# Four small edits at the front of an attention and two-layer feed-forward kernel: group sizes, order of the last sums, a constant as a column, a rounding step on another engine

## The chip, the cores and the metric

The kernel runs on one core of a Trainium2 chip. A core has five engines, each with its own in-order queue of instructions: TensorE (PE in the profile; PEld is its weight load), VectorE (DVE), ScalarE (ACT), GpSimd (POOL) and SyncE (SP), which here issues nearly all DMA transfers. They meet only through semaphores. The metric is the device time of one execution in microseconds, as the median of several runs; lower is better.

## The reference

Everything is float32. With x of 12480 tokens by 128 features and 32 inducing rows I:

```
h   = softmax(I x^T / sqrt(128)) x            # 32 x 128, a sum over all 12480 tokens
a   = softmax(x h^T / sqrt(128)) h            # 12480 x 128; both softmaxes divide by (sum + 1e-9)
u   = a w1a ;  y = (u * clip(u + 3, 0, 6) / 6) w1b     # 128 -> 2048 -> 128
v   = y w2a ;  out = (max(v, 0)^2) w2b                 # 128 -> 2048 -> 128
```

The weights come as 64-bit floats, which the kernel turns into float32 itself (pieces a, b, c, d of 512 columns, four of each, for w1a, w1b, w2a, w2b).

## The kernel before, in words

**First attention, the front of the program.** The first softmax is a sum over all tokens, so nothing of the second may start before it is complete. The tokens are cut into nine groups (GROUPS, L31) of 4 times as many tokens as their blocks add up to: 1, 2, 3, 4, 4, 4 blocks of 128, then a group of 304 (kept for later use), then 3 blocks, then 1. For each group g the transposed tokens come by DMA (load_group, L340). PE makes scores (L400), DVE their negated maximum (L404), ACT the exponents (exps, L412) with their sum. For groups 0 to 5, PE turns the tokens block by block to rows (turn_x, L422; four transposes to a block) and ACT copies them out (L427). Groups 6 to 8 (NATURAL) are not turned: their rows are loaded a second time in natural order (load_natural, L357 and L361; n6, n7 and n8 below). PE turns the exponents (turn_e, L439; DVE copies them, L440), then sums rows weighted by exponents (accumulate, L450; four matmuls to a block), and ACT copies each group's sum to hsb (L455).

Each matmul in float32 shows as two passes in the trace: a row `x8` of L450 is one block.

**The end of the first attention.** The groups have their own maxima, so their sums are weighted: pl is the sum of lengths (L535), pg the weighted sum over groups 0 to 7 (L538), hg its copy on ACT (L543), ph the sum of the last group's part (L546) and of hg (L551). A few matmuls keep PE busy (fill, L290), DVE multiplies by the reciprocal (ht, L553), and the scores of the second attention follow (ps, L634).

**Queues around it.** SP issues the loads in the order of LOADS (L38): groups, pieces of w1a, then n6, n7, n8, pieces of w1b, and so on. The row tiles of natural loads share a ring of three buffers, so n7 waits until the sums of group 4 have been made; n7 and n8 are two halves of one tile.

**Second attention and feed-forward.** The 25 chunks of up to 512 tokens are worked through in stages k, eight to a chunk, written out in program order by the last loop (L919). In stage k PE makes two first-layer products (up1, L748), ACT the relu of h + 3 (L762), DVE the gate (L763), and PE, two stages later, the second product (down1, L790 or L802); the second layer follows 11 stages behind. The second softmax of chunk c + 1 is spread over the stages of chunk c: scores, att_shift, att_exp (ACT, L662), att_norm (DVE: l, le, r, a), att_turn. For chunks 0 and 1 att_norm also splits a into a rounded part (L687) and the rest (L690), both on DVE; PE turns them (L707) and ACT copies them out (L712). The norm of chunk 0 stands ahead of the stages, that of chunk 1 in stage 4. The turning of the weights (L180, L184 and L255 on ACT, L216 and L228 on DVE, L193 and L245 on POOL) lies between the stages by the tables EARLY, LATER and BESIDE.

Of the kernel before, what the change touches and what calls it, by code (L numbers as in the profile page):

```python
# [10 lines left out]
F32 = mybir.dt.float32  # L11
# [5 lines left out]
ALU = mybir.AluOpType  # L17
AX = mybir.AxisListType
# [3 lines left out]
P = 128  # L22
CH = 512
SHORT = {23: 384, 24: 320}
EPS = 1e-09
# [2 lines left out]
RAISED = {(kind, q) for kind in "bcd" for q in range(4)} | {("a", 3)}  # L28


GROUPS = [(128,), (128,) * 2, (128,) * 3] + [(128,) * 4] * 3 + [(128, 128, 48), (128,) * 3, (128,)]  # L31
KEPT = 6
TURN_V = {}
NATURAL = {6: (6,), 7: (7, 8), 8: ()}
AHEAD = 6


# [33 lines left out]
def induced_attention_then_two_ffn(  # L71
# [11 lines left out]
    nc = tc.nc  # L83
    NT, D = x.shape
    M = indT.shape[1]
# [6 lines left out]
    J = P // M  # L92
    SCALE = 1.0 / math.sqrt(D)
    NG = len(GROUPS)
    run = [sum(blocks) for blocks in GROUPS]
    assert sum(run) * J == NT and D == P and J == 4
# [18 lines left out]
    sp = ctx.enter_context(tc.tile_pool(name="sp", bufs=2))  # L115
# [150 lines left out]
    def jobs(names, engine=None):  # L266
        last = None
        for name in names.split():
            item, what = (name[0], int(name[1])), name[3]
            if what == "h":  # L270
                upper(item)
            elif what == "r":
                round_off(item)
            elif what == "l":
                last = lower(item, engine or nc.vector)
            elif what == "3":
                third_stage(item)
            elif what == "s":
                shift(item)
            elif what == "m":  # L280
                last = merge(item)
            else:
                last = (first_stage if what == "1" else second_stage)(item) or last
        return last

    def fill(n, pool, tag, bufs, of=None):
        t = pool.tile([P, P], F32, tag=tag, name="fill", bufs=bufs)
        for i in range(n):
            if of is None:
                nc.tensor.transpose(t, ident, ident)  # L290
            else:
                nc.tensor.matmul(t, lhsT=of, rhs=of, start=True, stop=True)
# [3 lines left out]
    def tick():  # L296
        ticks.append(len(ticks))
        return jobs(EARLY.get(ticks[-1], ""))
# [13 lines left out]
    xg = {}  # L312
    ctx.enter_context(tc.manual_schedule())
    with ExitStack() as pro:
        pp = pro.enter_context(tc.tile_pool(name="pp", bufs=1))
# [8 lines left out]
        sel, ind, inds = (row[:, i, :] for i in range(3))  # L324
        xn = {}

        def load_group(g):
            n = run[g] * J
            if g == KEPT:
                xg[g] = xlast  # L330
            elif g == 0:
                t = pp.tile([P, n + run[1] * J], F32, tag="x01", name="xg")
                xg[0], xg[1] = t[:, :n], t[:, n:]
            elif g == NG - 1:
                xg[g] = pp.tile([P, n], F32, tag="x01", name="xg")
            elif g > 1:
                xg[g] = pp.tile([P, n], F32, tag="xg", name="xg", bufs=3)
            if g == 3:
                nc.vector.tensor_copy(xg[g][:, :1], inds[:, :1])
            nc.sync.dma_start(xg[g], xT[:, t0[g]:t0[g] + n])  # L340
            of = NATURAL.get(g, (g,))
            if not of:
                return
            n = sum(len(GROUPS[i]) for i in of)
            t = pp.tile([P, n * J, D], F32, tag="xn", name="xn", bufs=3)
            for i in of:
                xn[i], t = t[:, :len(GROUPS[i]) * J, :], t[:, len(GROUPS[i]) * J:, :]

        def whole_blocks(g):
            return sum(blk == P for blk in GROUPS[g])  # L350

# [13 lines left out]
        def load(item):  # L365
            kind, n = item
            if kind == "x":
                load_group(n)
            elif kind == "n":
                load_natural(n)  # L370
            else:
                load_piece(item)
# [8 lines left out]
            out=sel, in_=ident.rearrange("p (j i) -> p i j", j=J), axis=AX.X, op=ALU.add  # L381
        )
        nc.vector.tensor_reduce(
            out=blk4, in_=ident.rearrange("p (j i) -> p j i", j=J), axis=AX.X, op=ALU.add
# [6 lines left out]
        hsb = pp.tile([P, NG, D], F32, name="hsb")  # L391
# [25 lines left out]
        def turn_x(g, b):  # L417
            blk, o = GROUPS[g][b], sum(GROUPS[g][:b])
            t = pps.tile([blk, J, D], F32, tag="xt", name="xt", bufs=4)
            for j in range(J):  # L420
                i = j * run[g] + o
                nc.tensor.transpose(t[:, j, :], xg[g][:, i:i + blk], ident)  # L422
            dst = xn[g][:blk].rearrange("p (j b) d -> p b j d", j=J)[:, b]
            if b in TURN_V:
                nc.vector.tensor_copy(dst, t)
            else:
                nc.scalar.copy(dst, t)  # L427

        def turn_e(g):
# [3 lines left out]
            for b, blk in enumerate(GROUPS[g]):  # L433
                o, full = sum(GROUPS[g][:b]), whole_blocks(g)
                if g in NATURAL and b < full:
                    e = es[g][:, b:full * P:full]
# [8 lines left out]
        def accumulate(g, first=0, end=J):  # L445
            nb = len(GROUPS[g])
            acc = hacc[g % 2][:, g // 2 % 4, :]
            for b, blk in list(enumerate(GROUPS[g]))[first:end]:
                for j in range(J):
                    nc.tensor.matmul(  # L450
                        acc[M * j:M * (j + 1), :], lhsT=et[g][:blk, b, M * j:M * (j + 1)],
                        rhs=xn[g][:blk, j * nb + b, :], start=(b == 0), stop=(b == nb - 1),
                    )
            if end >= nb:
                nc.scalar.copy(hsb[:, g, :], acc)  # L455
# [37 lines left out]
        for g in range(NG - 1):  # L493
# [9 lines left out]
            for b in range(len(GROUPS[g])):  # L503
                if g not in NATURAL:
                    turn_x(g, b)
# [21 lines left out]
        tick()  # L527
        accumulate(NG - 2)
        tick()
        accumulate(NG - 1)  # L530
        rw, lws = weights[1:]

        pg = pps.tile([P, D], F32, tag="xt", name="pg", bufs=4)
# [2 lines left out]
        for g in range(NG - 1):  # L536
# [3 lines left out]
                start=(g < J), stop=(g + J >= NG - 1),  # L540
            )
        hg = pp.tile([P, D], F32, tag="sel4", name="hg")
        nc.scalar.copy(hg, pg)  # L543
        tick()
        ph = pps.tile([P, M], F32, tag="xt", name="ph", bufs=4)
        nc.tensor.matmul(ph, lhsT=hsb[:, NG - 1, :], rhs=rw[:, NG - 1, :], start=True, stop=False)  # L546
        den = pp.tile([P, M], F32, name="den")
        nc.vector.tensor_scalar_add(den, pl, EPS)
        rec = pp.tile([P, M], F32, name="rec")
        nc.vector.reciprocal(rec, den)  # L550
        nc.tensor.matmul(ph, lhsT=hg, rhs=sel, start=False, stop=True)  # L551
        fill(5, pps, "xt", 4)
        nc.vector.tensor_tensor(  # L553
            out=ht4, in0=ph.unsqueeze(1).to_broadcast([P, J, M]),
            in1=rec.unsqueeze(1).to_broadcast([P, J, M]), op=ALU.mult,
        )
        jobs("b0.s")


    hp = ctx.enter_context(tc.tile_pool(name="hp", bufs=3, space=PSUM))  # L560
    ap_ = ctx.enter_context(tc.tile_pool(name="accp", bufs=1, space=PSUM))
    wpool2 = ctx.enter_context(tc.tile_pool(name="wpool2", bufs=1))
# [95 lines left out]

    def att_exp(c):
        t = att.pop(c)  # L660
        e = sp.tile(list(t.shape), F32, tag="e", name="e")
        nc.scalar.activation(e, t, AF.Exp, scale=SCALE)  # L662
        att[c] = e

    def att_weights(c):
        e = att.pop(c)
        shape = list(e.shape)
        l = sp.tile(shape[:2], F32, tag="l", name="l")
        nc.vector.tensor_reduce(out=l, in_=e, axis=AX.X, op=ALU.add)
        le = sp.tile(shape[:2], F32, tag="le", name="le")  # L670
        nc.vector.scalar_tensor_tensor(
            out=le, in0=l, scalar=EPS, in1=l, op0=ALU.add, op1=ALU.max
        )
        r = sp.tile(shape[:2], F32, tag="r", name="r")
        nc.vector.reciprocal(r, le)
        a = sp.tile(shape, F32, tag="a", name="a")
        nc.vector.tensor_tensor(
            out=a, in0=e, in1=r.unsqueeze(2).to_broadcast(shape), op=ALU.mult
        )
        return a  # L680

    def att_norm(c):
        a = att_weights(c)
        att[c] = a
        if c < TURNS:
            a4 = sp.tile([P, J, 2, 2, M], F32R, tag="a4", name="a4", bufs=1)
            nc.vector.tensor_copy(  # L687
                a4[:, :, :, 0, :], a.unsqueeze(2).to_broadcast([P, J, 2, M])
            )
            nc.vector.tensor_tensor(  # L690
                out=a4[:, :, :, 1, :], in0=a.unsqueeze(2).to_broadcast([P, J, 2, M]),
                in1=a4[:, :, :, 0, :], op=ALU.subtract,
            )
            att[c] = a4
            return a4[:, 0, 1, 1, :1].bitcast(F32)
        return a[:, 0, :1]
# [203 lines left out]
    jobs("b0.m")  # L900
    mix(0)
    att_exp(0)
    mix_high(0)
    mix(1)
# [14 lines left out]
    for k in range(K + OFF + L2 + 1):  # L919
        c, p = divmod(k, NP)  # L920
# [78 lines left out]
```

## Time and profile before

| what | before |
|---|---|
| time, median of 3 runs | 949.58 us (949.49 to 949.62) |
| the profiled execution | 949.87 us, of which the span is 948.1 us |
| PE busy | 941.7 us, 99% |
| DVE busy | 787.5 us, 83% |
| ACT busy | 818.2 us, 86% |
| POOL busy | 261.7 us, 28% |
| granted TensorE clock | full in every slice |

The span runs from the first instruction to the last; 1.8 us of the time lie around it. The time falls into a front of about 35 us (first attention, bound by loads and PE in turns), a run-in to about 63 us in which the stages of the first layer start, and a long even part. The profile's chain of waits follows the end of the program back to its start, at each step to what released it; a view by stretches gives the busy time of each engine, and a DMA view the time from issue to landing.

### The profile page before, as it was taken

What the parts mean: (1) busy time and instruction counts of PE and PEld (TensorE: products, weight loads), DVE (VectorE), ACT (ScalarE), POOL (GpSimd) and SP (SyncE); (2) the same over time, 40 slices, a digit from 0 to 9 for tenths busy, and PEclk for the clock granted to TensorE, in tenths of its full rate; (3) what the DMA queues carried; (4) which work ended last, traced back from release to release, by engine and by line L of the source; (5) the groups of instructions that cost most, each with busy time, mean ns of one, the idle gap of its engine ahead of it and who ended that gap; (6) DMA issues with size and microseconds to landing.
All of it is one profiled execution on the core that took longest, in us unless ns stands there. A gap on an engine that the chain in (4) does not pass through costs nothing.

```text
span 948.1 us, 12829 instructions
## 1 busy us (share of the span) xinstructions
PE 941.7 (99%) x4578; PEld 763.7 (81%) x4578; DVE 787.5 (83%) x948; ACT 818.2 (86%) x937; POOL 261.7 (28%) x427
## 2 busy tenths in 40 slices
PE   9999999999999999999999999999999999999998
PEld 6556788888888888888888888888888888888898
DVE  5898788888888888888888888888888888888774
ACT  6789888888888888888888888888888888889886
POOL 1356222222222222222222223222222222222222
PEclk9999999999999999999999999999999999999999
DMA  9731000002000002000000000010000100000000
GB/s 351 280 89 56 23 1 22 10 14 68 8 16 23 6 19 67 4 20 23 1 22 27 30 24 10 13 56 8 15 23 7 44 23 4 20 20 4 16 12 16
DMA packets 31424, 35.43 MB, mean 37 GB/s; under 512 B 7489, under 2 KB 24705, under 8 KB 30977
## 3 DMA queue, kind: packets, MB, share of 16 engines
q1 hardware_dynamic: 31216, 34.60, 11.0%
q8 instruction: 36, 0.59, 0.3%
q14 instruction: 28, 0.22, 0.1%
q10 hardware_dynamic: 144, 0.02, 0.0%
HBM read 22.33 MB, written 6.39 MB: 30 GB/s over the span
## 4 chain that ended last, share of the span: by engine, by line
PE 97%; DVE 1%; DMA 1%; ACT 0%; issue 0%; SPq 0%
PE h L831 28%; PE oacc L802 27%; PE yacc L802 26%; PE h L748 9%; PE yacc L790 2%; PE oacc L790 1%; DMA xg<-in_xT 1%; PE xt L422 1%; PE hacc L450 1%; PE ps L604 1%; PE s L400 1%; DVE g L763 0%; PE ett L439 0%; ACT g L762 0%; PE ps L634 0%
## 5 line engine op out<-in xcount | busy, mean ns | idle before, releaser
L763 DVE SCALAR_TENSOR_TENSOR g<-g,h 128x1024 f32<-128x1024 f32 (+3 forms) x201 | 238.7, 1189 | 116.6 <-ACT g L762 113.8
L762 ACT ACTIVATE g<-h,small 128x1024 f32<-128x1024 f32 (+3 forms) x201 | 219.3, 1092 | 107.1 <-PE h L748 106.7
L866 DVE TENSOR_TENSOR lo<-g,hi 128x1024 fp32r<-128x1024 f32 (+3 forms) x193 | 229.2, 1188 | 7.8 <-PE oacc L802 4.1
L782 DVE TENSOR_TENSOR lo<-g,hi 128x1024 fp32r<-128x1024 f32 (+2 forms) x186 | 221.1, 1189 | 0.8 <-POOL hi L774 0.8
L846 ACT ACTIVATE g<-g 128x1024 f32<-128x1024 f32 (+3 forms) x201 | 206.1, 1026 | 0.2
L842 ACT ACTIVATE g<-h 128x1024 f32<-128x1024 f32 (+3 forms) x201 | 199.2, 992 | 3.3 <-PE h L831 2.1
L858 ACT CAST hi<-g 128x1024 fp32r<-128x1024 f32 (+1 forms) x186 | 191.7, 1031 | 0.0
L774 POOL TENSOR_SCALAR hi<-g 128x1024 fp32r<-128x1024 f32 (+2 forms) x184 | 190.9, 1038 | 0.6 <-DVE g L763 0.2
L831 PE MATMUL h<-yh,wh 128*128 128x512 f32 (+2 forms) x400 | 153.8, 384 | 0.0
L831 PE MATMUL h<-yh,wl 128*128 128x512 f32 (+2 forms) x400 | 153.7, 384 | 0.0
L831 PE MATMUL h<-yl,wh 128*128 128x512 f32 (+2 forms) x400 | 153.7, 384 | 0.0
L748 PE MATMUL h<-at,m 128*128 128x512 f32 (+2 forms) x400 | 129.2, 405 | 0.6 <-DVE g L763 0.4
L895 POOL COPY small<-lo 128x1 f32<-128x1 f32 x115 | 21.8, 189 | 344.5 <-DVE lo L782 344.5
L802 PE MATMUL oacc<-hi,wh 128*128 128x512 f32 (+2 forms) x384 | 116.5, 384 | 0.0
L802 PE MATMUL oacc<-hi,wl 128*128 128x512 f32 (+2 forms) x384 | 116.4, 384 | 0.0
L802 PE MATMUL oacc<-lo,wh 128*128 128x512 f32 (+2 forms) x384 | 116.4, 384 | 0.0
L802 PE MATMUL yacc<-hi,wh 128*128 128x512 f32 (+2 forms) x372 | 112.4, 383 | 0.0
L802 PE MATMUL yacc<-hi,wl 128*128 128x512 f32 (+2 forms) x372 | 112.4, 383 | 0.0
L802 PE MATMUL yacc<-lo,wh 128*128 128x512 f32 (+2 forms) x372 | 112.4, 383 | 0.0
L748 PEld LDWEIGHTS h<-at,m 128*128 128x128 f32 x400 | 74.4, 188 | 24.8 <-issue 7.7
L831 PEld LDWEIGHTS h<-yl,wh 128*128 128x128 f32 x400 | 75.1, 188 | 14.5
L831 PEld LDWEIGHTS h<-yh,wh 128*128 128x128 f32 x400 | 75.1, 188 | 14.5 <-DVE g L763 0.4
(126 smaller groups left out, 912.9 us busy)
## 6 DMA issues: line engine op xcount, KB each, us to landing
outT<-osb SPq DMA_DIRECT2D x23, 256.0 KB, 2.2
xc<-in_xT SPq DMA_DIRECT2D x9, 512.0 KB, 4.3
xg<-in_xT SPq DMA_DIRECT2D x3, 1024.0 KB, 7.9
at<-ah SPq DMA_DIRECT2D x168, 16.0 KB, 1.8
at<-al SPq DMA_DIRECT2D x168, 16.0 KB, 1.8
raw<-in_w1a SPq DMA_DIRECT2D x4, 512.0 KB, 8.6
raw<-in_w1b SPq DMA_DIRECT2D x4, 512.0 KB, 7.5
raw<-in_w2a SPq DMA_DIRECT2D x4, 512.0 KB, 8.3
```

The source lines that it names most:

```text
L748: nc.tensor.matmul(h1[k][u] if k == 0 else h1[k][:, u, :size[c]], lhsT=m4[:, f * P:(f + 1) * P], rhs=a_t[c], start=True, stop=True)
L762: nc.scalar.activation(g, h, AF.Relu, bias=three)
L763: nc.vector.scalar_tensor_tensor(out=g, in0=g, scalar=6.0, in1=h, op0=ALU.min, op1=ALU.mult)
L774: nc.gpsimd.tensor_scalar(out=hi1[k], in0=g1[k], scalar1=1.0, scalar2=1.0, op0=ALU.mult, op1=ALU.mult)
L782: nc.vector.tensor_tensor(out=lo1[k], in0=g1.pop(k), in1=hi1[k], op=ALU.subtract)
L790: nc.tensor.matmul(acc, lhsT=w[:, f * P:(f + 1) * P], rhs=g[u] if isinstance(g, list) else g[:, u, :], start=(p == 0 and u == 0), stop=(p ...
L802: nc.tensor.matmul(acc, lhsT=w[:, f * P:(f + 1) * P], rhs=g[:, u, :], start=(p == 0 and n == 0), stop=(p == NP - 1 and n == 5),)
L831: nc.tensor.matmul(h2[k][:, u, :size[c]], lhsT=w, rhs=y, start=(n == 0), stop=(n == 2))
L842: nc.scalar.activation(g2[k][:, u, :], h[:, u, :n], AF.Relu)
L846: nc.scalar.activation(g2[k][:, u, :], g2[k][:, u, :], AF.Square)
L858: nc.scalar.copy(hi2[k][:, u, :], g2[k][:, u, :])
L866: nc.vector.tensor_tensor(out=lo2[k][:, u, :], in0=g[:, u, :], in1=hi2[k][:, u, :], op=ALU.subtract)
```

## The change

There are four edits.

1. GROUPS: the third group has two blocks instead of three, the last but one four instead of three. The natural rows of groups 7 and 8 no longer share a tile: group 8's rows lie behind its transposed tokens in a tile of the first groups' buffer.
2. The sums of the last group (accumulate of group 8) are written behind pg and hg instead of ahead of pl, and the two matmuls into ph change places.
3. In chunk 0 of the second attention the exponents lie in a tile with one more column that holds the constant 1e-9, and the reduction runs over it; the step that added the constant goes.
4. In chunk 1 the rounding of a is a copy on ScalarE instead of VectorE.

```diff
-GROUPS = [(128,), (128,) * 2, (128,) * 3] + [(128,) * 4] * 3 + [(128, 128, 48), (128,) * 3, (128,)]
+GROUPS = [(128,), (128,) * 2, (128,) * 2] + [(128,) * 4] * 3 + [(128, 128, 48), (128,) * 4, (128,)]
-NATURAL = {6: (6,), 7: (7, 8), 8: ()}
+NATURAL = {6, 7, 8}
...
             elif g == NG - 1:
-                xg[g] = pp.tile([P, n], F32, tag="x01", name="xg")
+                t = pp.tile([P, 2 * n], F32, tag="x01", name="xg")
+                xg[g], xn[g] = t[:, :n], t[:, n:].rearrange("p (b d) -> p b d", d=D)
...
-            of = NATURAL.get(g, (g,))
-            if not of:
-                return
-            n = sum(len(GROUPS[i]) for i in of)
-            t = pp.tile([P, n * J, D], F32, tag="xn", name="xn", bufs=3)
-            for i in of:
-                xn[i], t = t[:, :len(GROUPS[i]) * J, :], t[:, len(GROUPS[i]) * J:, :]
+            if g < NG - 1:
+                xn[g] = pp.tile([P, len(GROUPS[g]) * J, D], F32, tag="xn", name="xn", bufs=3)
...
-        accumulate(NG - 1)
         rw, lws = weights[1:]
...
         nc.scalar.copy(hg, pg)
+        accumulate(NG - 1)
         tick()
         ph = pps.tile([P, M], F32, tag="xt", name="ph", bufs=4)
-        nc.tensor.matmul(ph, lhsT=hsb[:, NG - 1, :], rhs=rw[:, NG - 1, :], start=True, stop=False)
...
-        nc.tensor.matmul(ph, lhsT=hg, rhs=sel, start=False, stop=True)
+        nc.tensor.matmul(ph, lhsT=hg, rhs=sel, start=True, stop=False)
+        nc.tensor.matmul(ph, lhsT=hsb[:, NG - 1, :], rhs=rw[:, NG - 1, :], start=False, stop=True)
...
+    e0 = sp.tile([P, J, M + 1], F32, tag="e", name="e0")
+    nc.vector.memset(e0[:, :, M:], EPS)
...
-        e = sp.tile(list(t.shape), F32, tag="e", name="e")
+        if c:
+            e = sp.tile(list(t.shape), F32, tag="e", name="e")
+        else:
+            e = e0[:, :, :M]
...
-        l = sp.tile(shape[:2], F32, tag="l", name="l")
-        nc.vector.tensor_reduce(out=l, in_=e, axis=AX.X, op=ALU.add)
         le = sp.tile(shape[:2], F32, tag="le", name="le")
-        nc.vector.scalar_tensor_tensor(
-            out=le, in0=l, scalar=EPS, in1=l, op0=ALU.add, op1=ALU.max
-        )
+        if c:
+            l = sp.tile(shape[:2], F32, tag="l", name="l")
+            nc.vector.tensor_reduce(out=l, in_=e, axis=AX.X, op=ALU.add)
+            nc.vector.scalar_tensor_tensor(
+                out=le, in0=l, scalar=EPS, in1=l, op0=ALU.add, op1=ALU.max
+            )
+        else:
+            nc.vector.tensor_reduce(out=le, in_=e0, axis=AX.X, op=ALU.add)
...
-            nc.vector.tensor_copy(
-                a4[:, :, :, 0, :], a.unsqueeze(2).to_broadcast([P, J, 2, M])
-            )
+            rounding = nc.scalar.copy if c else nc.vector.tensor_copy
+            rounding(a4[:, :, :, 0, :], a.unsqueeze(2).to_broadcast([P, J, 2, M]))
```

On PE, at the end of the first attention, the order before was this (hacc is the sums of L450, `x12` the three blocks of group 7, the `x4` behind it the block of group 8):

```order
L439 MATMUL ett<-ident,es 128x128
L450 MATMUL hacc_122<-xn,et 32x128 x12
L450 MATMUL hacc_121<-xn,et 32x128 x4
L535 MATMUL pl<-row,lws 128x32
L538 MATMUL pg<-hsb,rw 32x128 x8
L546 MATMUL ph<-rw,hsb 128x32
L551 MATMUL ph<-row,hg 128x32
L290 MATMUL fill<-ident 128x128 x5
```

In the changed program the same place on PE reads:

```order
L435 MATMUL ett<-ident,es 128x128
L446 MATMUL hacc_122<-xn,et 32x128 x16
L530 MATMUL pl<-row,lws 128x32
L533 MATMUL pg<-hsb,rw 32x128 x8
L446 MATMUL hacc_121<-xg,et 32x128 x4
L546 MATMUL ph<-row,hg 128x32
L547 MATMUL ph<-rw,hsb 128x32
L290 MATMUL fill<-ident 128x128 x5
```

Group 7 has a block more, the block of group 8 stands behind pg, and the part of hg now opens ph.

On ACT, in the stages around chunk 1's norm, the order before was this (g is the relu of a stage, stage 4 first; cva, cve and wh are steps of the weights; at is the turned a of chunk 1):

```order
L762 ACTIVATE g_737<-h_734,small 128x1024
L762 ACTIVATE g_756<-h_753,small 128x1024
L180 ACTIVATE cva<-raw 128x512
L184 ACTIVATE cve<-raw 128x512
L255 CAST wh<-w_642 128x512
L762 ACTIVATE g_778<-h_775,small 128x1024
L255 CAST wh<-w_680 128x512
L712 CAST at<-pt 128x512
```

In the changed program ACT has there:

```order
L765 ACTIVATE g_730<-h_727,small 128x1024
L692 CAST a_743<-a 128x8x32
L765 ACTIVATE g_749<-h_746,small 128x1024
L180 ACTIVATE cva<-raw 128x512
L184 ACTIVATE cve<-raw 128x512
L255 CAST wh<-w_635 128x512
L765 ACTIVATE g_771<-h_768,small 128x1024
L255 CAST wh<-w_673 128x512
```

The rounding of a stands behind the relu of stage 4 and ahead of that of stage 5 and the steps of the weights.

## Rows read from the trace of the kernel before

**Rows 1.** The page: busy time (share of the span) and instructions of each engine.

```profile
PE 941.7 (99%) x4578; PEld 763.7 (81%) x4578; DVE 787.5 (83%) x948; ACT 818.2 (86%) x937; POOL 261.7 (28%) x427
```

**Rows 2.** Stretches: length, then busy us of PE, PEld, DVE, ACT, POOL; clock, DMA.

```profile
52.00:56.00 4.00, 3.60 (x14) 1.99 (x13) 4.00 (x6) 3.23 (x6) 1.41 (x2) 1.00 0.11 22
56.00:60.00 4.00, 4.00 (x11) 1.78 (x10) 4.00 (x6) 2.68 (x5) 2.04 (x3) 1.00 0.85 238
100.00:200.00 100.00, 100.00 (x458) 80.39 (x457) 84.24 (x97) 86.33 (x93) 26.54 (x44) 1.00 0.06 17
```

**Rows 3.** The chain of waits in order of time: start us, us, what.

```profile
1.64 7.53 DMA xg<-in_xT
...
9.31 0.85 PE s L400 x8
...
10.53 1.31 PE xt L422 x12
...
30.40 1.01 PE hacc L450 x32
...
31.75 0.64 PE pg L538 x16
...
32.41 0.27 ACT hg L543
...
32.73 0.41 PE ph L551 x2
33.14 0.59 PE fill L290 x5
...
36.21 0.17 DVE le L671
...
51.22 0.59 DVE a L687
...
56.36 3.58 PE yacc L790 x8
```

**Rows 4.** SP's issues of n6's second part, then n7 and n8.

```profile
20.99 0.50 SPq L361 DMA_DIRECT2D xn<-in_x  x1
25.30 0.94 SPq L357 DMA_DIRECT2D xn<-in_x  x2
```

**Rows 5.** DMA issues: n7, and n6's second part; KB, us from issue to landing.

```profile
xn<-in_x SPq DMA_DIRECT2D x1, 768.0 KB, 4.5
...
xn<-in_x SPq DMA_DIRECT2D x1, 96.0 KB, 6.8
```

**Rows 6.** Stretches of one microsecond; the last two columns are DMA share and GB/s.

```profile
23.00:24.00 1.00, 1.00 (x15) 0.71 (x17) 0.93 (x3) 1.00 (x4) 0.00 (x0) 1.00 1.07 413
25.00:26.00 1.00, 1.00 (x16) 0.58 (x12) 0.40 (x2) 1.00 (x3) 0.17 (x1) 1.00 0.77 254
26.00:27.00 1.00, 1.00 (x11) 0.34 (x3) 0.88 (x2) 1.00 (x5) 1.00 (x1) 1.00 0.70 151
```

**Rows 7.** ACT in order of time: start, us, instruction, [idle before <- releaser].

```profile
35.54 0.31 ACT L662 ACTIVATE e<-t 128x128 f32<-128x128 f32 x1 [0.59 <-DVE t L653]
...
47.43 2.27 ACT L762 ACTIVATE g<-h,small 128x1024 f32<-128x1024 f32 x2
...
50.74 0.60 ACT L255 CAST wh<-w 128x512 fp32r<-128x512 f32 x1
...
53.09 0.58 ACT L712 CAST at<-pt 128x512 fp32r<-128x512 f32 x1 [0.23 <-PE pt L707]
54.22 1.11 ACT L762 ACTIVATE g<-h,small 128x1024 f32<-128x1024 f32 x1 [0.55 <-PE h L748]
...
58.61 1.14 ACT L255 CAST wh<-w 128x512 fp32r<-128x512 f32 x2 [1.10 <-POOL w L245]
```

**Rows 8.** DVE in order of time, the gates of stages 6 to 8.

```profile
54.25 1.21 DVE L763 SCALAR_TENSOR_TENSOR g<-g,h 128x1024 f32<-128x1024 f32 x1
...
56.69 2.34 DVE L763 SCALAR_TENSOR_TENSOR g<-g,h 128x1024 f32<-128x1024 f32 x2
```

## The prediction

> **What bounds the kernel now.** I read the page first: TensorE (PE) is busy for nearly the whole span [rows 1]. Then the table of stretches: from 100 us on PE works without a gap, while ScalarE (ACT) and VectorE (DVE) keep some 15% of slack, and the edits touch nothing there; between 52 and 60 us PE already loses 0.40 us, DVE is full, and ACT has 0.77 and 1.32 us idle [rows 2]. So a microsecond won or lost at the front goes one to one into the end. Third came the chain of waits in order of time [rows 3], which is where the terms are read: PE waits for the third group's load until 9.31, then works through to the sums that begin at 30.40, then the short pieces PE, ACT, PE that make h, a row of small DVE steps (le, a, ...), and a DVE stretch around 51 us before PE takes over again. Last I read the times of the natural loads [rows 4, 5], the DMA engines by microsecond [rows 6], and ACT and DVE around 50 us [rows 7, 8].
>
> **Part 1: third group of two blocks, last but one of four.** The load of x2 shrinks from 768 to 512 KB. Four transposes and one evacuation go (12 transposes take 1.31, so 4 take 0.44), and the sums of one block go (the row of 16 blocks' sums that follows 30.40 counts 32 passes, 8 to a block of four matmuls, so four blocks 1.01 and one 0.25) [rows 3]; group 7 gets that block's sums back. Through PE alone the sums of group 7 could begin earlier by 0.65 (x2, see below) + 0.44 + 0.25 + some 0.2 (an estimate: a third of the 0.85 that the third group's scores take, less about as much as group 7's grow by): 1.55 us, at 28.85 rather than 30.40.
>
> But group 7 isn't transposed: its rows come by a load of their own, which grows from 768 KB to 1 MB. It is 256 KB more in the one queue, and nothing ahead of it in the queue gets smaller in sum, because x7 takes back what x2 gives up. In the trace the part of n6 that was issued last (20.99) lands 6.8 later, at 27.79; n7, issued at 25.30, lands 4.5 later, at 29.80 [rows 4, 5]: 768 KB in 2.0 us behind n6, so 256 KB cost 0.65. Before, the sums wait 0.6 us beyond that landing, so it is hidden by that much only. From 25 to 27 us the queues run half empty (254 and 151 GB/s against 413 before), yet n6 still lands only at 27.8 [rows 6]: some of the 16 engines had finished and the last ones had not. The landing of n7 is that of the latest engine, which has no gap to fill, however early n7 is issued. So n7 lands at 29.80 + 0.65 = 30.45; with the 0.14 that lay between landing and first matmul for x2 (1.64 + 7.53 = 9.17, then 9.31 [rows 3]) the sums start at 30.59, 0.19 later than before. If instead the idle engines took the extra bytes, n7 would land at its old 29.8 and the sums start at 29.94. I take the first value, since n6 was late while engines stood idle.
>
> The Trainium skill, page "DMA: Bandwidth & Descriptors", section "Why a DMA increments its semaphore by 16 and not by 1", says that a transfer runs on up to 16 engines that finish independently and only the full count means that all has landed; the half-empty microseconds agree. The same page, "Measured (HBM→SBUF, 128 partitions, SWDGE, issued from GpSimd)", has the opposite pull: transfers of 1 MiB and more come nearer to peak, so four blocks would cost less than pro rata and two blocks more. No row here shows a gain by size in a full queue; by that rule the landing would move towards the second value.
>
> **Part 2: the last group's sums behind the weighted ones.** Counted from the start s of group 7's sums. Before: sums 1.01 (three blocks of group 7 and one of group 8), pl, then pg from s + 1.35 to s + 1.99, hg on ACT s + 2.01 to 2.28, ph until 33.14 = s + 2.74, the fills 0.59, next step at s + 3.37 [rows 3]. After: all four blocks belong to group 7 and stand ahead of pg, so pg still ends at s + 1.99; the block of group 8 (0.25) lies beside hg. That hides it, but its copy to SBUF on ACT now stands behind hg (s + 2.28 + 0.02 + 0.25 = s + 2.55) and the last ph matmul waits for it: s + 2.60 + 0.41 = s + 3.01. That is 0.27 later than before, which takes back all that the cover gives, so the added block is paid in full. n8 lands some 0.65 behind n7, before s + 1.99, so it isn't late; hsb of group 7 is ready while pg does its first seven matmuls. ACT's weight rounding queued behind that copy slides by the same amount; it ended 0.6 before the exponent, which waited for DVE that long, so it stays hidden.
>
> Front in sum: 0.19 + 0.27 = 0.46 us later at the first attention scores; −0.2 by the other value of the landing; −1.3 (28.85 − 30.40 + 0.27) if no load is late at all.
>
> **Part 3: the small constant as a column.** One DVE step on the chain goes: 0.17 + 0.02 = 0.19 us [rows 3]. Four more columns beside 128 lengthen the reduction by a thirtieth at most; the memset falls into DVE's wait for the scores. Bounds: −0.19, and 0 if the odd row pitch of e slows its three readers.
>
> **Part 4: second chunk rounded by ScalarE.** DVE loses a CAST of 0.59 [rows 3]. ACT gains one. Its price isn't in the trace for 256 columns: the exponent of 128 columns takes 0.31 and a CAST of 512 columns 0.60 [rows 7], so 0.41. What matters is its place. By the order it stands right behind the relu of stage 4 and ahead of the relu of stage 5. Its input a is ready on DVE at 51.2. Before, ACT ran two relus from 47.43 on (2.27 for both [rows 7]): the first ends at 48.55, the second is stage 5's, which DVE wants only after both of its rounding steps, the first of which ends at 51.81; then came weight rounding until 51.3 and stage 6's relu. After, ACT stands still from 48.55 to 51.2, 2.65 us, with all of that queued behind. Stage 5's relu starts at 51.2 + 0.41 = 51.6 instead of 48.57: ACT is 3.05 late. Its idle time from 52 to 60 is 0.77 + 1.32 = 2.09 [rows 2], so some 0.96 is left at 60 us. The path through DVE agrees: stage 7's relu moves from 54.22, less its wait of 0.55 and the 0.23 before it, by 3.05 to 56.5, ends at 57.6; DVE by then has done stage 6 (56.6 instead of 55.46 [rows 8]) and its two weight steps (55.46 to 56.69 before) at 57.85, does stage 7's product until 59.05 instead of 57.86, and PE's second half of the x8 row, which ended at 59.94 [rows 3], starts at 59.1 and ends at 60.9. I take +0.95. Bounds: below, −0.17, if ACT had nothing that anyone waits for (0.59 + 0.02 saved, 0.02 + 0.41 + 0.01 waited); above, the whole 3.05.
>
> **Sum against the profiled execution** (949.87 us, of which the span is 948.1 and 1.77 lies around it): 0.46 − 0.19 + 0.95 = +1.22. The median of the runs shown is 949.58, 0.29 below the profiled one; on it the forecast is 949.58 + 1.22 = 950.8 us. Less than about 0.2% (1.9 us) can't be told from no change, so the forecast is "same", on the slow side.
>
> **Rivals.**
> A. The extra natural bytes are taken by idle engines, n7 is in time; the rest as forecast: −0.2 − 0.19 + 0.95 = +0.56, 950.1. For it: the half-empty microseconds. Against: n6 lands late in spite of them.
> B. The lag of the latest engine is made during x2's load and goes with the smaller x2; no load is late: −1.3 − 0.19 + 0.95 = −0.54, 949.0. For it: at 0.65 per 256 KB the 1536 KB of x0 to x2 would take 3.9 us, and x2 lands only at 9.17, so some 3 us are lost there. Against: the bytes up to n7 are more, not fewer.
> C. ACT's standstill is free, because DVE is the bound of that stretch: 0.46 − 0.19 − 0.17 = +0.1, 949.7. Against: DVE itself needs the relu of stage 5 next. With B it would be −1.66, 947.9.
> D. The other side, slower by more than can be missed: ACT's standstill is not absorbed. Its idle stretches between 52 and 60 are waits for PE and GpSimd work that itself comes later, so they move along, and from 60 us on ACT has no slack that PE doesn't need. Then all 3.05 stay: 0.46 − 0.19 + 3.05 = +3.3, 952.9. It decides if PE still waits for stage 9's product when it comes back from stage 7. Against: stage 7 waited 0.55 for PE and a weight rounding 1.1 us for GpSimd, neither of which comes 3 us later.
>
> **How the numbers follow.** Forecast 0.50 (its own range 950.2 to 951.4: the landing 0.3 either way, the ACT term 0.5 to 1.4), A 0.20, B 0.08, C 0.08, D 0.12, something else 0.02. The forecast, A, C and most of B are within 0.2%; B with C is at the edge of faster; D and the upper tail are slower. Faster 0.03, same 0.84, slower 0.13. The range leaves out half of B and most of D: 949.2 to 952.2.
>
> **What would show it.** Right: x2 lands some 0.65 earlier and PE starts the third group's scores near 8.7; then PE idles ahead of group 7's sums with n7 as the releaser, landing near 30.4; ph's last matmul waits for ACT; no le step in the first chunk; an ACT gap of over 2 us ahead of the CAST, released by DVE a; DVE then waits for ACT's relu, and PE idles some 1 us more than before between 53 and 60. Wrong: group 7's sums start at 30 or earlier (A or B), no gap on ACT ahead of the CAST, or PE still behind by 3 us at 70 (D).

## The result: slower by 0.64%, outside the range

| | before | after |
|---|---|---|
| median, measured together (6 runs each) | 949.54 us (949.20 to 949.62) | 955.43 us (955.25 to 956.46) |
| ratio, 95% interval | | 1.0064 [1.0051, 1.0077] |
| profiled execution (span) | 949.87 us (948.1) | 956.46 us (954.7) |

The change costs 5.9 us by the medians and 6.6 us between the two profiled executions, of which the one after is the slowest of its six; 950.8 us was predicted, with 952.2 as the upper end. To find where the time goes, I take the start of ACT's relu of the same stage in both traces, each counted from the start of its span, after less before, and call it the shift. It is +0.29 us in stage 0, +3.24 in stage 5, +1.21 in stage 9, +1.20 in stage 14, +1.73 in stage 15, +1.71 in stage 23, +6.83 in stage 183 and +6.64 in the last. So there are three losses: 0.29 at the front, 1.45 at the run-in (0.92 until stage 9, 0.53 at stage 15), and 4.9 that come a little at a time in the even part. The first is within what the front varies by from one execution to the next (see the end of the experiments).

The page after, as [rows 1]: PE is as full as before, with 4 us more work by the clock and four instructions fewer.

```profile
PE 946.0 (99%) x4574; PEld 762.6 (80%) x4574; DVE 787.0 (82%) x947; ACT 818.4 (86%) x937; POOL 261.3 (27%) x427
```

**The front.** PE in order of time: the sums of group 7, with the idle time before them and its releaser.

```profile
30.55 0.71 PE L446 MATMUL hacc<-xn,et 128*32 128x128 f32 x17 [1.20 <-DMA xn<-in_x]
```

The chain of waits in order of time, as [rows 3]: start, us, what.

```profile
23.30 7.12 DMA xn<-in_x
...
30.55 1.08 PE hacc L446 x32
...
31.97 0.67 PE pg L533 x16
...
32.66 0.27 ACT hg L538
...
32.98 0.41 PE ph L546 x2
33.39 0.22 PE ph L547 x2
33.62 0.59 PE fill L290 x5
...
36.36 0.30 DVE le L677
...
36.69 0.19 DVE r L679
```

PE stands idle for 1.20 us until n7 lands at 23.30 + 7.12 = 30.42; ph now comes in two pieces, of which the second ends 0.48 us later than the one piece of [rows 3] (fill at 33.62 against 33.14); and in chunk 0 the reciprocal follows directly on the reduction.

**The run-in.** ACT in order of time, as [rows 7]:

```profile
47.73 1.13 ACT L765 ACTIVATE g<-h,small 128x1024 f32<-128x1024 f32 x1
51.52 0.40 ACT L692 CAST a<-a 128x256 fp32r<-128x256 f32 x1 [2.66 <-DVE a L681]
51.83 1.11 ACT L765 ACTIVATE g<-h,small 128x1024 f32<-128x1024 f32 x1
```

Between the relus of stages 4 and 5 ACT stands still for 2.66 us, until DVE has made a, and then rounds it. The table of stretches shows what PE loses by it, first before, then after (columns as in [rows 2]):

```profile
50.00:55.00 5.00, 4.60 (x16) 2.38 (x15) 4.83 (x11) 4.22 (x7) 1.82 (x4) 1.00 0.34 102
70.00:75.00 5.00, 5.00 (x18) 3.01 (x17) 3.94 (x5) 5.00 (x8) 3.89 (x5) 1.00 0.08 20
```

```profile
50.00:55.00 5.00, 4.10 (x15) 2.32 (x14) 3.84 (x9) 3.48 (x6) 1.70 (x2) 1.00 0.32 105
70.00:75.00 5.00, 4.50 (x14) 2.38 (x14) 4.39 (x8) 5.00 (x7) 3.26 (x6) 1.00 0.05 13
```

PE idles 0.90 us of the first stretch instead of 0.40, and 0.50 of the second, where before it was full.

**The even part.** One stage on PE begins with the pair of first-layer matmuls, `h<-at,m`. Before, two such pairs in sequence, and what follows the first:

```profile
402.41 0.62 PE L748 MATMUL h<-at,m 128*128 128x512 f32 x2
402.86 0.39 PE L831 MATMUL h<-yh,wh 128*128 128x512 f32 x1
...
404.22 0.61 PE L802 MATMUL yacc<-hi,wh 128*128 128x512 f32 x2
...
406.94 0.61 PE L748 MATMUL h<-at,m 128*128 128x512 f32 x2
```

The same after:

```profile
406.12 0.63 PE L751 MATMUL h<-at,m 128*128 128x512 f32 x2
406.59 0.39 PE L834 MATMUL h<-yh,wh 128*128 128x512 f32 x1
...
407.97 0.61 PE L805 MATMUL yacc<-hi,wh 128*128 128x512 f32 x2
...
410.69 0.63 PE L751 MATMUL h<-at,m 128*128 128x512 f32 x2
```

A stage takes 4.57 us instead of 4.53, with no idle time and the same instructions. All of it lies between the pair and yacc: 1.85 us (407.97 − 406.12) instead of 1.81. The groups of instructions between 200 and 800 us (busy us, mean ns of one), before and then after:

```profile
L748 PE MATMUL h<-at,m 128*128 128x512 f32 x262 | 81.2, 391 | 0.0
...
L831 PE MATMUL h<-yh,wl 128*128 128x512 f32 x262 | 102.0, 389 | 0.0
```

```profile
L834 PE MATMUL h<-yh,wl 128*128 128x512 f32 x262 | 103.5, 395 | 0.0
...
L751 PE MATMUL h<-at,m 128*128 128x512 f32 x261 | 82.5, 396 | 0.0
...
L805 PE MATMUL oacc<-hi,wh 128*128 128x512 f32 x260 | 80.0, 389 | 0.0
```

No edit touches these matmuls. What differs is where their operand lies: tile at is at byte 137728 of each partition before and at 137664 after, 64 bytes lower, by the addresses in the two built programs. Edit 3 is why: chunk 0 no longer takes a tile l, so the allocator first meets l in chunk 1 and puts it behind at instead of ahead of it. yh, yl, hi, lo and the weights lie where they lay. With 160 stages from 23 to 183, the growth of the shift, 6.83 − 1.71 = 5.12 us, is 0.032 a stage.

### The profile page after: what moved, and what is told of

Read it like the earlier page. It is cut to its first block, busy times and chain, and to the rows that moved or that the text cites. A ratio compares the mean times of both kernels' runs of the same rounds, so it can differ in the third digit from the quotient of the medians.

```text
span 954.7 us, 12817 instructions
## 1 busy us (share of the span) xinstructions
PE 946.0 (99%) x4574; PEld 762.6 (80%) x4574; DVE 787.0 (82%) x947; ACT 818.4 (86%) x937; POOL 261.3 (27%) x427
## 4 chain that ended last, share of the span: by engine, by line
PE 95%; DMA 2%; DVE 2%; ACT 1%; issue 0%; SPq 0%; ACTq 0%
PE h L834 28%; PE oacc L805 27%; PE yacc L805 26%; PE h L751 9%; PE oacc L793 1%; PE yacc L793 1%; DMA xg<-in_xT 1%; DVE g L766 1%; DMA xn<-in_x 1%; PE ps L602 1%; ACT g L765 0%; PE xt L418 0%; DMA row<-in_indT 0%; PE hacc L446 0%; PE s L396 0%
```

## The experiments

Every kernel below was timed against the kernel before on the same chip; three chips were used, so each time stands beside its own time before. Three things were to be told apart: whether the place of at is the cause of the loss in the even part, whether ACT's standstill is that of the run-in, and what the other edits do.

**The change with l kept in chunk 0**, which puts at back at 137728:

```diff
         le = sp.tile(shape[:2], F32, tag="le", name="le")
+        l = sp.tile(shape[:2], F32, tag="l", name="l")
         if c:
-            l = sp.tile(shape[:2], F32, tag="l", name="l")
```

> The changed kernel with one line more: the small tile l is also taken in chunk 0 (nobody uses it there), so that the tile at (the turned weights that the first-layer matmuls read) lies where it lay before, at byte 137728 of a partition, a multiple of 512, and not 64 bytes lower. Every instruction is the same. Theory P (place): in the changed trace each even stage is 4.567 us long against 4.533, all of the 34 ns in the eight matmuls from the two that read at; over some 155 stages that is 5.2 us. With at back the stage is 4.533 again and the time 955.4 - 5.2 = 950.2 us. Rival T (time): ACT's standstill put the engines out of step and the stages never come back into it; then the place does nothing and the time stays 955.4. Rival O: it is the order of e, nm and t, which this kernel leaves as changed; also 955.4.

Measured: 950.62 us against 949.26, ratio 1.0018 [1.0009, 1.0027]. The shift is constant, +0.75, from stage 17 to the end. The groups, 200 to 800 us:

```profile
L751 PE MATMUL h<-at,m 128*128 128x512 f32 x262 | 81.2, 391 | 0.0
```

The mean is that of before. A tile of 16 bytes that chunk 0 takes and doesn't use (with its second buffer and the spacing, 64 bytes) returns the even part; what is left, 1.36 us by the medians, is near the 1.22 that the prediction had for the whole change.

**The kernel before with l alone moved** out of its ring in chunk 0, so that at lies 64 bytes lower; no other line is changed (le, r, a, a4 and st, which stand between l's old place and its new one, move down with it):

```diff
-        l = sp.tile(shape[:2], F32, tag="l", name="l")
+        l = sp.tile(shape[:2], F32, tag="l" if c else "nm", name="l")
```

> The kernel before with the reverse: l takes, in chunk 0 alone, a buffer of nm's ring, so its own is first taken in chunk 1, behind at; at lies 64 bytes lower, at 137664, as in the changed kernel. No instruction changes. P: 949.5 + 5.2 = 954.7 us, stages of 4.567. T and O: 949.5 us.

Measured: 954.21 us against 949.26, ratio 1.0050 [1.0035, 1.0065]. The shift is +0.16 at the front, +0.21 in stage 15 and +5.12 at the end, so 4.91 come behind stage 15. Two pairs in sequence, and the group:

```profile
400.03 0.63 PE L748 MATMUL h<-at,m 128*128 128x512 f32 x2
...
404.60 0.63 PE L748 MATMUL h<-at,m 128*128 128x512 f32 x2
```

```profile
L748 PE MATMUL h<-at,m 128*128 128x512 f32 x260 | 82.1, 396 | 0.0
```

Stage length, mean and the 4.91 us are those of the changed kernel. So the move of these tiles alone makes the whole loss of the even part, without any of the four edits; at is the only one of them that the matmuls of an even stage read.

**Other distances.** l and le both moved (at 128 bytes lower), and a tile of 32 bytes that restores half of the distance (at 32 lower):

```diff
-        le = sp.tile(shape[:2], F32, tag="le", name="le")
+        le = sp.tile(shape[:2], F32, tag="le" if c else "nm", name="le")
```

> As the last one, with le moved likewise: at lies 128 bytes lower than in the kernel before, at 137600, a multiple of 128 but not of 256 or 512. P with a grid of 128 bytes or less: 949.5 us, stages of 4.533. P with a coarser grid (256 or 512): about 954.7 us again. T and O: 949.5 us.

```diff
-        l = sp.tile(shape[:2], F32, tag="l", name="l")
+        l = sp.tile(shape[:2], F32, tag="l" if c else "nm", name="l", bufs=1 if c else 2)
...
+            if c == 0:
+                gap = sp.tile([P, 8], F32, tag="gap", name="gap", bufs=1)
```

> The kernel before with at 32 bytes lower (l's own buffers behind at, one of them only, and an unused tile of 32 bytes ahead), at byte 137696. No instruction changes. Measured so far: 64 bytes lower makes an even stage 4.567 us and the time 954.2 (950.6 with at back), 128 bytes lower 4.553 and 952.2. P as 'any place off a multiple of 512 costs': a stage of 4.55 to 4.57 again, 951.5 to 954.5. P as 'only the 64-byte half counts, the 128 run was something else': 4.533 or 4.567, nothing between.

Measured: 952.18 us (ratio 1.0029 [1.0018, 1.0040]) at −128 and 952.82 (1.0035 [1.0022, 1.0048]) at −32; a stage takes 4.55 us in both. Every distance tried costs, and not in proportion to it: 64 bytes cost most.

**The second layer's tiles moved instead**, at left in place. A gap ahead of their pool moves yh, yl, g2, hi and lo of the second layer, by 64, 128 and 256 bytes:

```diff
+    gap = ep2.tile([P, 16], F32, tag="gap", name="gap", bufs=1)   # 16, 32 or 64 columns
     def up1(k):
```

> The kernel before with at in its old place, but all moving operands of the second layer (yh, yl, hi, lo) 64 bytes higher, by an unused tile ahead of them. If a place off the 512 grid slows any matmul that reads there, the twelve second-layer matmuls of a stage (six of h, six of oacc) slow down instead of the first ones: the two of at cost 34 ns, so twelve cost up to 200 ns a stage and the time is up to 30 us longer; slower by over 5 us in any case. If it is something of at alone (its DMA writers, say): 949.5.

> As the run with the second layer's moving operands 64 bytes higher (+13.7 us, stages 4.620), now 128. If the cost is that of a place off a multiple of 512: slower again, stages of 4.57 to 4.64, 955 to 965. If a multiple of 128 is enough: 949.7 (the 128-byte shift of at cost 20 ns a stage, which speaks against).

> The same with 256 bytes. Grid of 512: slower, stages over 4.55, 952 to 965. Grid of 256: 949.7, stages of 4.533.

Measured: 963.34 us at +64 (1.0145 [1.0131, 1.0159]), 961.91 at +128 (1.0135 [1.0122, 1.0149]) and 949.47 at +256 (1.0001 [0.9992, 1.0010]). The second layer's second product, between 200 and 800 us, at +64 and at +256:

```profile
L803 PE MATMUL oacc<-hi,wh 128*128 128x512 f32 x258 | 81.2, 396 | 0.0
```

```profile
L803 PE MATMUL oacc<-hi,wh 128*128 128x512 f32 x264 | 81.3, 389 | 0.0
```

So it isn't the move but the address: all operands that stream through these matmuls lay at multiples of 512 bytes, a shift by 256 is free, and every smaller one costs. It isn't particular to at either. At +64 a stage takes 4.62 us; 12 of its 20 matmuls read moved tiles, and the loss is 0.09.

**Edit 4 alone** in the kernel before:

```diff
-            nc.vector.tensor_copy(
-                a4[:, :, :, 0, :], a.unsqueeze(2).to_broadcast([P, J, 2, M])
-            )
+            rounding = nc.scalar.copy if c else nc.vector.tensor_copy
+            rounding(a4[:, :, :, 0, :], a.unsqueeze(2).to_broadcast([P, J, 2, M]))
```

> The kernel before with the fourth edit alone (chunk 1's rounding on ScalarE); at stays at 137728. By the prediction ACT stands still for 2.65 us and +0.95 us is left: 950.5. The changed trace lost 0.9 at stage 10 and 0.54 more at stage 16: if both come from the standstill, +1.45: 951.0. T: the stages get out of step and the even part drifts, some +5 to +6: 955. If ACT's standstill is absorbed: 949.4.

Measured: 950.33 us against 949.26, ratio 1.0011 [1.0002, 1.0021]. ACT and the two stretches:

```profile
46.34 1.11 ACT L761 ACTIVATE g<-h,small 128x1024 f32<-128x1024 f32 x1
50.11 0.40 ACT L688 CAST a<-a 128x256 fp32r<-128x256 f32 x1 [2.66 <-DVE a L677]
```

```profile
50.00:55.00 5.00, 4.09 (x14) 2.04 (x12) 3.89 (x6) 4.89 (x8) 1.79 (x3) 1.00 0.28 79
70.00:75.00 5.00, 4.51 (x16) 2.61 (x15) 3.74 (x5) 5.00 (x8) 3.86 (x5) 1.00 0.09 22
```

The same gap, and the same two losses on PE. The shift goes from −1.09 in stage 4 to −0.19 in stage 9 and +0.34 from stage 15 to the end: 0.90, then 0.53. In the even part it stays where it is. Both losses of the run-in are edit 4's.

**Edit 4 written later**: the same copy on ACT, but in stage 5, behind that stage's relu and two weight steps (att_round is att_norm from the rounding on). DVE's step that takes the rest of a goes along with it, and the weight step b3.2 now stands behind both.

```diff
+        if k == 5:
+            jobs("c0.1 b0.h")
+            att_round(1)
+            last = jobs("b3.2") or last
```

> The kernel before with the fourth edit at another place: chunk 1's rounding is on ScalarE, but written in stage 5, behind that stage's relu and two weight steps, where its input is ready when ACT comes to it; the rest (DVE) stands behind the gate of stage 5. ACT does the same work as in the run with edit 4 alone (+1.1). If the standstill is the cause: no gap ahead of the CAST, and 949.6, the time of before. If it is ACT's added work or PE's later turn: +1.1 again, 950.7.

Measured: 949.28 us against 949.40, ratio 0.9999 [0.9990, 1.0008]. ACT and the stretches:

```profile
49.52 0.60 ACT L255 CAST wh<-w 128x512 fp32r<-128x512 f32 x1
50.02 0.40 ACT L694 CAST a<-a 128x256 fp32r<-128x256 f32 x1
50.33 1.10 ACT L766 ACTIVATE g<-h,small 128x1024 f32<-128x1024 f32 x1
```

```profile
50.00:55.00 5.00, 4.85 (x17) 2.62 (x16) 5.00 (x8) 4.70 (x9) 1.91 (x4) 1.00 0.48 145
70.00:75.00 5.00, 4.99 (x18) 2.99 (x17) 2.95 (x4) 5.00 (x7) 3.33 (x5) 1.00 0.10 26
```

No gap, and PE full in the second stretch. In the profiled execution the shift even falls, from −1.24 in stage 4 to −1.59 in stage 9, and then stays; the medians don't show that 0.35. The copy's work on ACT costs nothing that can be seen; with its early place go the gap and a loss of 1.4 us within the profiled execution, 1.07 us by the medians. What the later DVE step and b3.2 do by themselves wasn't run.

**The other edits.** Edits 1 to 3 with l kept (the first experiment with the rounding back on DVE), edit 3 alone with l kept, and edit 3 with l kept together with edit 4 written later:

```diff
-            rounding = nc.scalar.copy if c else nc.vector.tensor_copy
+            rounding = nc.vector.tensor_copy
```

> The changed kernel with l taken in chunk 0 (at in its old place) and the rounding of chunk 1 back on VectorE: edits 1, 2 and 3 alone. By the prediction +0.46 from the natural load and the tail and -0.19 for the missing step: +0.27, 949.5. Rival A or B (n7 in time, lag gone): -0.4 to -1.5, 948 to 949. From the runs with at back (950.6) less what edit 4 cost alone (+1.1): about the time of before.

> The kernel before with the third edit alone, at in its old place: one DVE step of 0.19 us fewer on the chain. Prediction: -0.19, so 0.02% faster, at the edge of what can be seen among front-end differences of 1 us from run to run; the profile should show the stages 0.2 us earlier counted from the last ph matmul. If the odd pitch of e costs its readers: 0.

> The kernel before with the third edit and the fourth at its later place, at where it was: -0.2 for the missing DVE step, 0 to -0.2 for the rounding off DVE: 949.3, that is 0.03% faster, if anything can be seen of it.

Measured: 949.55 us against 949.67 (1.0004 [0.9993, 1.0016]; one of the eleven runs took 955.49), 949.41 against 949.67 (0.9996 [0.9987, 1.0005]) and 948.95 against 949.40 (0.9995 [0.9986, 1.0004]). None can be told from the kernel before; the last has the lowest median, and whether it is better stays open.

The front varies from one execution to the next, also where its code is the same. The chain of the kernel with edit 4 alone begins like this; [rows 3] has 7.53 for the same load.

```profile
1.64 6.00 DMA xg<-in_xT
7.64 0.14 issue
7.77 0.85 PE s L400 x8
```

No edit touches this load, yet it lands 1.5 us earlier, and the shift in stage 0 is −1.12. Two more traces hold the changed front, the change with l kept and edits 1 to 3: their shift in stage 0 is −0.69 and −0.36, where the changed kernel has +0.29. Medians of the kernel before went from 949.26 to 949.67 between the chips, single runs from 948.39 to 950.55. So terms of the front, 0.2 to 0.5 us, can't be read from the times, and of the traces only steps counted from the step before them, not from the start.

## Why the prediction was wrong

**The step that failed is Part 3.** It priced the constant's column by its instructions alone, between −0.19 and 0 us. The instruction did go and saved its 0.19. But the edit also drops a tile in chunk 0, the tiles behind it move down by 64 bytes, and the first-layer matmuls of all later stages slow down: 4.9 us, where the upper bound was 0. With it falls the sentence in the first part that from 100 us on the edits touch nothing: they change no instruction there, but an address. No rival held it, since all of them dealt with waits and landings; the range was built from those and so ended at 952.2. The list of the tiles' addresses in the two built programs, which needs no run, would have shown the move; its price took runs.

The Trainium skill, page "SBUF — State Buffer", section "Operand start alignment", asks of an operand's address only that it be a multiple of the element's size, and says of itself that this is about legality and not about speed. The runs agree, and add the price: every address tried was legal, and 5 of 6 were slower.

**Part 1's numbers came out, partly by luck.** n7 was put at 30.45 and landed at 30.42, the sums at 30.59 and began at 30.55. The argument was that idle engines take nothing, however early n7 is issued. But n7 was issued 2.00 us earlier than before (23.30 against 25.30), and the dip that the argument rests on [rows 6] shrank; after the change (columns as there):

```profile
25.00:26.00 1.00, 1.00 (x31) 0.80 (x34) 1.00 (x4) 0.97 (x3) 0.32 (x2) 1.00 0.94 261
26.00:27.00 1.00, 1.00 (x27) 0.80 (x16) 1.00 (x3) 0.67 (x3) 0.40 (x1) 1.00 1.05 389
```

The queues moved 261 and 389 GB/s there instead of 254 and 151, and n7 was late all the same. In the other two traces of this front, first the change with l kept, then edits 1 to 3, the sums of group 7 began at:

```profile
29.58 1.08 PE L446 MATMUL hacc<-xn,et 128*32 128x128 f32 x32 [0.84 <-DVE rw L484]
```

```profile
29.91 1.08 PE L446 MATMUL hacc<-xn,et 128*32 128x128 f32 x32 [1.17 <-DVE cve L228]
```

Each time that is 0.14 us behind n7's landing (29.44 and 29.77), as forecast, though in these two the profile names DVE as the releaser. But 29.94 was rival A's value, and in the eleven traces with the old front the sums begin anywhere from 28.99 to 30.45. So that PE idles ahead of these sums until about n7's landing holds in three of three; that this start comes 0.19 later than before isn't shown, and rival A is neither shown nor out. By the Trainium skill, "DMA: Bandwidth & Descriptors", section "Why a DMA increments its semaphore by 16 and not by 1", only the full count of engines means that all data is there; no view here shows the engines one by one. Of rival B the first half holds: x2 with two blocks landed at 7.08 to 7.20 in three traces, with three blocks at 7.63 to 9.17 in eleven, so the third group's scores began at 7.58 and not near 8.7. The second half, no load late, doesn't: PE stood idle for 0.84 to 1.20 us ahead of the sums.

**Part 2 had the size and not the wait.** It gave ph 0.27 more than the start of the sums; the fills begin 0.48 later, of which 0.15 are the sums' start, so 0.33. But the last ph matmul doesn't wait for ACT's copy of group 8's sums, which is done at 33.10:

```profile
32.83 0.27 ACT L451 COPY hsb<-hacc 128x128 f32<-128x128 f32 x1
```

It follows straight on the one for hg, which ends at 33.39 in the chain. What costs is that matmul itself, 0.22 us that stood ahead of hg before and stands behind it now. With the 0.19 of the step saved, stage 0 was expected 0.27 later and is 0.29 later in this pair of traces, which is luck, given the −0.69 and −0.36 above. The 0.19 itself is firm: from the first fill to the first relu it is 6.45 to 6.46 us in all five traces with the column and 6.64 to 6.66 in the nine without.

**Part 4 was right in its mechanism and short by a term.** The gap on ACT was put at 2.65 us and is 2.66, the copy at 0.41 and takes 0.40, and ACT was put 3.05 late in stage 5: the shift grows by 2.95 there. What is left was put at 0.95 near 60 us and is 0.92 in stage 9. But the delay wasn't paid in full there: PE loses another 0.53 us, which ACT shows from stage 15 on. I had followed the delay to the x8 row of yacc and taken what PE got back as absorbed. Rival C, a free standstill, is out. Rival D had the idea (not absorbed) but not the size: 1.45 of the 3.05 us stay. That it stems from the standstill is shown by edit 4 alone, which has it, and by the copy written later, which hasn't. DVE carries it: in the chain after, DVE goes without a pause from 65.48 through a gate, two weight steps, a second gate and the whole norm of chunk 2 to a third gate, whose end PE waits for. That gate before, then after, then PE:

```profile
70.18 1.21 DVE L763 SCALAR_TENSOR_TENSOR g<-g,h 128x1024 f32<-128x1024 f32 x1
```

```profile
71.39 1.21 DVE L766 SCALAR_TENSOR_TENSOR g<-g,h 128x1024 f32<-128x1024 f32 x1
```

```profile
72.66 0.50 PE L834 MATMUL h<-yh,wh 128*128 128x512 f32 x1 [0.50 <-DVE g L766]
```

The gate is 1.21 us later, and PE, which before had no idle time from 70 to 75 us, now waits 0.50 us for it.

**The sum.** Between the profiled executions: 0.29 (forecast 0.27) + 0.92 (0.95) + 0.53 (0) + 4.91 (0) = 6.65 us, against 954.7 − 948.1 = 6.6 of the spans. By the medians the moved tile alone costs 4.95 us and edit 4 alone 1.07, together 6.02, against 5.89 for the whole change. Each of these has an interval of about a microsecond either way, so the medians bear out the two large terms and say nothing of the front.

## What to carry to other kernels

An edit that adds or drops a tile, however small, moves others: compare the addresses of the operands that stream through the hot matmuls before asking what an edit costs, and keep them on multiples of 256 bytes, or of 512, which is all that was tried for at. On an in-order engine the place of an instruction whose input comes late can matter more than its own time, as edit 4 showed (950.33 us in the early place, 949.28 in the late one); move it behind work that is ready. And a delay followed to one point of the program isn't absorbed until the next place where PE meets that engine is checked too.

## What was not expected of the hardware

The address of an operand that streams through a matmul of 128x512 float32 sets its pace. At multiples of 256 bytes (all at multiples of 512, or the second layer's moved by 256) a stage of 20 matmuls takes 4.53 us. Where at is the only one of these operands that moved, 32 and 128 bytes lower give 4.55, 64 lower 4.57; with the second layer's tiles 64 or 128 higher it is 4.62 and 4.61. The cost isn't confined to matmuls that read the moved tile: after the change `h<-yh,wl`, which comes two matmuls behind the pair and reads a tile that lies where it lay, goes from 389 to 395 ns, while the twelve matmuls into yacc and oacc stay at 389. What in the chip makes it so, no run here shows.
